# Attention and mixture of experts on one core: each head's k loaded on both halves of the rows, and q and k split in place

## The chip, the cores and the metric

The kernel runs on one core of a Trainium2 chip. The metric is the device time of one execution in microseconds; lower is better. Five engines work side by side, each through its own list of instructions in order: TensorE (PE, whose weight loads stand as PEld), VectorE (DVE), ScalarE (ACT), GpSimd (POOL), and SyncE (SP), which here issues nearly all DMAs. An instruction that waits for a semaphore holds up everything behind it on its engine.

## The reference

For 8 batches of 12 heads (448 positions, head size 64) a causal attention is computed in float32; its output, as 3584 rows of 768, goes to a mixture of 8 experts that picks one expert for each row and keeps the 80 rows with the largest gate for each.

```python
scores = scale * np.matmul(q, k.transpose(0, 1, 3, 2))
scores = np.where(mask, -1000000000.0, scores)
attn = np.exp(scores - np.max(scores, axis=-1, keepdims=True))
attn = attn / (np.sum(attn, axis=-1, keepdims=True) + 1e-09)
x = np.matmul(attn, v)            # then as (8 * 448, 768)
expert_idx = np.argmax(x @ w_gate, axis=1)
for e in range(8):
    tok_idx = the 80 rows of expert e with the largest gate_w
    out[tok_idx] = gate_w[tok_idx, None] * (np.maximum(x[tok_idx] @ w1[e], 0.0) @ w2[e])
```

## The kernel before

The heads are worked in **pairs**: 6 pairs in a batch, 48 in all, numbered 0 to 47 from here on. A pair has its even head's 64 components in SBUF rows 0 to 63 (`lo`) and its odd head's in rows 64 to 127 (`hi`). Loads and splits go by **thirds** of a batch, which are two pairs (`PH = 2`): 24 thirds. Third h is loaded two thirds ahead by `load_third` and split during third h-1 by the steps of `split_third`.

The splitting is there because a score is computed from float16 parts: q and k are each cut into a high part (the float16 rounding) and a low part (what is left). For the even head, `qa` holds q's high part in rows 0 to 63 and its low part in rows 64 to 127; `ka` holds k's high part in both halves, `la` k's low part in both halves. One matmul of `qa` with `ka` and one with `la` then give all four products. `qb`, `kb` and `lb` are the same for the odd head. These six tiles are double buffered.

In the kernel before, `by_dma` makes them so: ACT rounds q into `qh` (L331) and DVE rounds k into `kh` (L336), whole tiles of 128 rows by 896; DMAs inside SBUF copy the halves of `qh` to `qa` and `qb` (L332, L333) and those of `kh` twice each to `ka` and `kb` (L338, L339). POOL computes q's low parts from `qh` straight into `qa` and `qb` (L342, L343) and k's low part into `kl` (L347), and four more DMAs copy `kl` to `la` and `lb` (L351, L352). `qh`, `kh` and `kl` have one buffer each. The first pair of third 0 is split by `at_once` with compute instructions alone.

Each pair has 8 **slots**, and the order on every engine is written by hand. In slots 0 to 6 PE makes a block of scores (L375, L376; the last block L385 to L388), DVE masks it and takes the row minimum (L397), and ACT takes the exponential (L400); in slots 0, 2, 4 and 6 PE also transposes four blocks of the pair before (L417), which ACT or DVE copies out (L429). In slot 7 PE multiplies the transposed weights of two pairs before with v (L445). There are three score buffers and two transpose buffers in PSUM. A dictionary `plan` adds steps to the end of a slot: `THIRD` gives the slots of the split, counted from slot 1 of the first pair of a third, and `NORMS`, `ROWS0`, `ROWS1` and `STEPS` those of the gate and the choice of rows for the batch before, whose small operations run on POOL and DVE (for instance L625, which subtracts the largest logit, and L674, the one-hot rows that PE needs). `late_constants` puts a run of POOL instructions ahead of the split in pair 4.

After the last pair comes the choice for the last batch, then the two layers of the experts with weights streamed from HBM. SP issues in one list: the loads of q, k and v, the copies inside SBUF, the stores of attention rows (`xs`, L582), the weights that are loaded ahead (L189), and the zeroing of the output (`out<-zero`, L271).

Of the kernel before, what the change touches and what calls it, by code (L numbers as in the profile page):

```python
# [38 lines left out]
def attention_then_moe(  # L39
# [24 lines left out]
    assert NT == 4 and LAST == QB and D == NP * P  # L64
# [131 lines left out]
    wg_sb = const.tile([P, NP, E], F32, name="wg_sb")  # L196
    tiny = const.tile([P, 1], F32, name="tiny")
    nc.gpsimd.memset(tiny, 1e-9)
    lg = keep.tile([P, NT, H * E], F32, name="lg")
    if LAST < P:  # L200
        nc.vector.memset(lg[LAST:P, NT - 1, :], 0.0)

    def late_constants():
# [53 lines left out]
        zero = const.tile([P, D // 2], F32, name="zero")  # L257
        nc.gpsimd.memset(zero, 0.0)
# [41 lines left out]
    def split_third(h):  # L300
# [5 lines left out]
        one = lambda n: apool.tile([P, PH, S], F16, name=n, tag=n, bufs=1)  # L306
        for nm in ("qa", "qb", "ka", "kb", "la", "lb"):
            st[nm] = t16(nm)
        qa, qb, ka, kb, la, lb = (st[nm] for nm in ("qa", "qb", "ka", "kb", "la", "lb"))

        def at_once(x):

            nc.scalar.copy(ka[lo, x], kf[lo, x])
            nc.vector.tensor_copy(qa[lo, x], qf[lo, x])
            nc.scalar.copy(ka[hi, x], kf[lo, x])  # L315
            nc.vector.tensor_tensor(out=qa[hi, x], in0=qf[lo, x], in1=qa[lo, x], op=ALU.subtract)
            nc.scalar.copy(qb[hi, x], qf[hi, x])
# [2 lines left out]
            nc.scalar.copy(kb[hi, x], kf[hi, x])  # L320
            nc.scalar.copy(kb[lo, x], kf[hi, x])
            nc.vector.tensor_tensor(out=qb[lo, x], in0=qf[hi, x], in1=qb[hi, x], op=ALU.subtract)
            nc.vector.tensor_tensor(out=lb[lo, x], in0=kf[hi, x], in1=kb[hi, x], op=ALU.subtract)
            nc.vector.tensor_tensor(out=lb[hi, x], in0=kf[hi, x], in1=kb[hi, x], op=ALU.subtract)

        def by_dma(x):
            st["qh"], st["kh"] = qh, kh = one("qh"), one("kh")
            kl = one("kl")

            def q_hi():  # L330
                nc.scalar.copy(qh[:, x], qf[:, x])  # L331
                nc.sync.dma_start(qa[lo, x], qh[lo, x])  # L332
                nc.sync.dma_start(qb[hi, x], qh[hi, x])  # L333

            def k_hi():
                nc.vector.tensor_copy(kh[:, x], kf[:, x])  # L336
                for t, rows in ((ka, lo), (kb, hi)):
                    nc.sync.dma_start(t[lo, x], kh[rows, x])  # L338
                    nc.sync.dma_start(t[hi, x], kh[rows, x])  # L339

            def q_lo(i):
                nc.gpsimd.tensor_tensor(out=qa[hi, i], in0=qf[lo, i], in1=qh[lo, i], op=ALU.subtract)  # L342
                nc.gpsimd.tensor_tensor(out=qb[lo, i], in0=qf[hi, i], in1=qh[hi, i], op=ALU.subtract)  # L343

            def k_lo(i):
                eng = nc.gpsimd if h else nc.vector
                eng.tensor_tensor(out=kl[:, i], in0=kf[:, i], in1=kh[:, i], op=ALU.subtract)  # L347

            def spread():
                for t, rows in ((la, lo), (lb, hi)):  # L350
                    nc.sync.dma_start(t[lo, x], kl[rows, x])  # L351
                    nc.sync.dma_start(t[hi, x], kl[rows, x])  # L352
# [953 lines left out]
```

## Time and profile before

| what | us |
|---|---|
| median of 3 runs (lowest to highest) | 525.53 (523.63 to 528.52) |
| the profiled execution, its own time | 528.05 |
| its span, first to last instruction | 526.3 |
| PE busy in the span | 463.1 (88%) |
| DVE busy | 410.8 (78%) |
| ACT busy | 391.7 (74%) |
| POOL busy | 211.5 (40%) |

The shares are averages over stages that have different limits: the attention takes the first 365 us of the span, the choice for the last batch some 30, the experts the rest. TensorE's granted clock was 0.97 of full speed on average. The ends of matmuls are modelled, so a busy PE may still be waiting a little.

### The profile page before, as it was taken

The numbers are of one execution on the slowest core, as the hardware profiler recorded it, in microseconds if no ns is written. First come the engines' busy times: TensorE is split into PE (matmuls) and PEld (weight loads), VectorE is DVE, ScalarE is ACT, GpSimd is POOL, SyncE is SP. The second block draws the span as 40 slices with busy tenths as digits, with TensorE's granted clock in tenths as the row PEclk, the third lists the DMA queues.
The fourth block names the chain that finished last, engine by engine and source line by source line (L and its number), as shares of the span: only waits on it lengthen the run. The fifth ranks groups of instructions, "written<-read, shape, count | busy, mean of one in ns | idle before, by whom it ended". The sixth has DMA issues, their size and how long they took to land. (4 is left out here: it accounts for less than half of the span.)

```text
span 526.3 us, 14874 instructions
## 1 busy us (share of the span) xinstructions
PE 463.1 (88%) x5247; PEld 354.7 (67%) x5247; DVE 410.8 (78%) x1286; ACT 391.7 (74%) x1048; POOL 211.5 (40%) x294
## 2 busy tenths in 40 slices
PE   2687979979799999999999999999959898999985
PEld 1355736756576667667667667777547898999984
DVE  5566738866697798789889789889387999988771
ACT  4787748866687788788789778878164898978670
POOL 4477424544443654565445445460005155300010
PEclk9999879998899999999999999999978999999998
DMA  6775898788888888989988988983297999999920
GB/s 198 191 192 168 233 273 246 206 239 247 259 251 230 265 249 266 282 259 267 292 251 254 272 260 264 277 249 133 84 381 242 370 392 390 398 423 421 420 84 22
DMA packets 63947, 136.85 MB, mean 260 GB/s; under 512 B 8786, under 2 KB 50770, under 8 KB 60416
## 3 DMA queue, kind: packets, MB, share of 16 engines
q1 hardware_dynamic: 62816, 132.39, 78.1%
q0 software_dynamic: 1056, 3.51, 2.0%
q8 instruction: 41, 0.67, 0.5%
q14 instruction: 34, 0.28, 0.2%
HBM read 85.35 MB, written 23.99 MB: 208 GB/s over the span
## 5 line engine op out<-in xcount | busy, mean ns | idle before, releaser
L400 ACT ACTIVATE prob<-ns,nb 128x128 f32<-128x128 f32 (+3 forms) x336 | 176.9, 529 | 33.4 <-DVE nb L397 32.0
L397 DVE CUSTOM_DVE_ANT_0 ns<-sp,mask 128x384 f32<-128x384 f32 (+2 forms) x288 | 117.1, 416 | 57.9 <-PE sp L376 46.1
L417 PE MATMUL tp<-ident,prob 128*128 128x128 f32 x768 | 120.7, 281 | 0.8 <-ACT PT L429 0.7
L429 ACT COPY PT<-tp 128x512 f32<-128x512 f32 x144 | 82.9, 576 | 43.7 <-PE tp L417 29.3
L1083 DVE SCALAR_TENSOR_TENSOR wl<-wraw,wh 128x768 f16<-128x768 f32 (+1 forms) x94 | 93.8, 1062 | 11.4 <-ACT wh L1098 8.1
L417 PEld LDWEIGHTS tp<-ident,prob 128*128 128x128 f32 x768 | 91.0, 144 | 15.5 <-ACT PT L429 6.8
L342 POOL TENSOR_TENSOR qa<-qf,qh 64x448 f16<-64x448 f32 x47 | 49.1, 1045 | 123.4 <-ACT qh L331 115.1
L445 PE MATMUL xp<-PT,vt 128*64 128x448 f32 (+3 forms) x768 | 92.1, 380 | 0.0
L1098 ACT ACTIVATE wh<-wraw 128x768 f16<-128x768 f32 (+1 forms) x94 | 80.9, 923 | 5.5 <-DMA wraw<-w 1.8
L445 PEld LDWEIGHTS xp<-PT,vt 128*64 128x64 f32 x768 | 54.3, 137 | 43.6 <-issue 23.2
L1158 PEld LDWEIGHTS <-wl 128*128 128x128 f16 x640 | 64.4, 101 | 5.0 <-issue 3.1
L1155 PEld LDWEIGHTS <-wh 128*128 128x128 f16 x640 | 65.0, 102 | 3.5 <-issue 3.1
L1157 PEld LDWEIGHTS <-wh 128*128 128x128 f16 x640 | 64.5, 101 | 1.7 <-issue 1.6
L400 ACT ACTIVATION_READ_ACCUMULATOR prob<-ns,nb 128x1 f32 x336 | 63.9, 190 | 0.0
L376 PE MATMUL sp<-la,qa 128*128 128x128 f16 x144 | 40.7, 283 | 18.4 <-DMA la<-kl 18.0
L343 POOL TENSOR_TENSOR qb<-qf,qh 64x448 f16<-64x448 f32 x47 | 48.9, 1041 | 3.4
L1211 POOL DMA_INDIRECT out<-yo,idx x8 | 19.0, 2374 | 77.3 <-ACT yo L1208 67.4
L347 POOL TENSOR_TENSOR kl<-kf,kh 128x448 f16<-128x448 f32 x46 | 46.9, 1040 | 1.8
L375 PE MATMUL sp<-kb,qb 128*128 128x128 f16 x144 | 40.4, 280 | 7.2 <-DVE nb L397 6.4
L375 PE MATMUL sp<-ka,qa 128*128 128x128 f16 x144 | 40.8, 283 | 6.7 <-ACT ka L315 5.2
L376 PE MATMUL sp<-lb,qb 128*128 128x128 f16 x144 | 40.4, 281 | 5.5 <-DMA lb<-kl 4.5
L1158 PE MATMUL op<-hh,wl 128*128 128x80 f16 x336 | 39.4, 204 | 3.0 <-DVE wl L1083 1.5
(187 smaller groups left out, 952.2 us busy)
## 6 DMA issues: line engine op xcount, KB each, us to landing
wraw<-w SPq DMA_DIRECT2D x27, 1536.0 KB, 20.3
out<-zero SPq DMA_DIRECT2D x56, 192.0 KB, 2.4
qf<-q_t SPq DMA_DIRECT2D x23, 448.0 KB, 4.7
kf<-k_t SPq DMA_DIRECT2D x23, 448.0 KB, 6.1
vt<-v_t SPq DMA_DIRECT2D x24, 384.0 KB, 6.6
xs<-xr SPq DMA_DIRECT2D x48, 192.0 KB, 2.3
wraw<-w SPq DMA_DIRECT2D x24, 256.0 KB, 3.2
ka<-kh SPq DMA_DIRECT2D x46, 112.0 KB, 4.8
```

The costliest lines, as they stand in the source:

```text
L375: nc.tensor.matmul(sp[:, 0:w], qx[:, p, t * P:w], kx[:, p, 0:w], start=True, stop=False)
L376: nc.tensor.matmul(sp[:, 0:w], qx[:, p, t * P:w], lx[:, p, 0:w], start=False, stop=True)
L397: pr.masked = nc.vector.tensor_tensor_reduce(out=ns[:, 0:w], in0=sp[:, 0:w], in1=m, scale=-1.0 / 8.0, scalar=HUGE, op0=ALU.add, op1=ALU.mi ...
L400: nc.scalar.activation(pr.P[:, off:off + w], ns[:, 0:w], AF.Exp, bias=nb, scale=-1.0, accum_out=total)
L417: nc.tensor.transpose(pr.tp[:, i], pr.P[:, off:off + P], ident)
L429: copy(dst, src)
L445: state["pe"] = nc.tensor.matmul(xp[rows, 0:w], st["vt"][:, c, p * P + j * DH:p * P + (j + 1) * DH], pr.PT[:, j, n0:n0 + w], start=(c == 0 ...
L1083: return nc.vector.scalar_tensor_tensor(out=l, in0=src, scalar=SW, in1=h, op0=ALU.mult, op1=ALU.subtract)
L1098: nc.scalar.activation(h, src, AF.Copy, scale=SW)
L1155: nc.tensor.matmul(o, wh[:, ws], ah[:, c, :], start=(x == 0 and i % per == 0), stop=False, skip_group_check=True)
L1157: nc.tensor.matmul(o, wh[:, ws], al[:, c, :], start=False, stop=False, skip_group_check=True)
L1158: nc.tensor.matmul(o, wl[:, ws], ah[:, c, :], start=False, stop=(x == n - 1), skip_group_check=True)
```

## The change

k is loaded twice: `kfa` holds the even head's k in both halves of the rows and `kfb` the odd head's, by four loads of 64 rows where there was one of 128. q's high part is rounded by ACT straight into its place in `qa` and `qb` (two instructions of 64 rows by 896 instead of one of 128 rows). DVE rounds `kfa` into `ka` and `kfb` into `kb` (two instructions of 128 by 896 instead of one). POOL subtracts `la` and `lb` in full (two instructions of 128 by 448 for each pair instead of one). The ten copies by DMA inside SBUF and the tiles `qh`, `kh` and `kl` are gone. The order of the steps is now q's low part, then k's low part, for the first pair of the third, and then the same for its second pair. The numbers in `THIRD` move with it; two transposes of rows (`ROWS1`), the first step of `NORMS` and one of `STEPS` move by a few slots. `wg_sb` becomes a view of `lg`, `zero` a view of `mask_l`.

```diff
-NORMS = [1, 2, 2]
+NORMS = [0, 2, 2]
...
-ROWS1 = [59, 62, 64, 67]
+ROWS1 = [59, 65, 65, 67]
...
-THIRD = [0, 0, 2, 3, 4, 6, 8]
+THIRD = [1, 1, 2, 2, 4, 5, 8]
...
-        zero = const.tile([P, D // 2], F32, name="zero")
-        nc.gpsimd.memset(zero, 0.0)
+        zero = mask_l[:, 0:D // 2]
...
-        st["qf"], st["kf"] = qf, kf = t32("qf"), t32("kf")
+        st["qf"], st["kf"] = qf, kf = t32("qf"), [t32("kfa"), t32("kfb")]
...
             nc.sync.dma_start(qf[:, x], qT[b, :, ps, :])
-            nc.sync.dma_start(kf[:, x], kT[b, :, ps, :])
+            for j, rows in enumerate((lo, hi)):
+                nc.sync.dma_start(kf[j][lo, x], kT[b, rows, ps, :])
+                nc.sync.dma_start(kf[j][hi, x], kT[b, rows, ps, :])
...
-        def by_dma(x):
-            st["qh"], st["kh"] = qh, kh = one("qh"), one("kh")
-            kl = one("kl")
...
+        def by_turns(x):
+            def q_high():
+                nc.scalar.copy(qa[lo, x], qf[lo, x])
+                nc.scalar.copy(qb[hi, x], qf[hi, x])
+
+            def k_high(j):
+                nc.vector.tensor_copy(k_hi[j][:, x], kf[j][:, x])
+
+            def q_low(i):
+                nc.gpsimd.tensor_tensor(out=qa[hi, i], in0=qf[lo, i], in1=qa[lo, i], op=ALU.subtract)
+                nc.gpsimd.tensor_tensor(out=qb[lo, i], in0=qf[hi, i], in1=qb[hi, i], op=ALU.subtract)
+
+            def k_low(i):
+                for j in range(2):
+                    nc.gpsimd.tensor_tensor(out=k_lo[j][:, i], in0=kf[j][:, i], in1=k_hi[j][:, i], op=ALU.subtract)
             each = range(x.start, x.stop)
-            return [q_hi, k_hi] + [lambda i=i: q_lo(i) for i in each] + [lambda i=i: k_lo(i) for i in each] + [spread]
+            return [q_high, lambda: k_high(0), lambda: k_high(1)] + [f for i in each
+                                                                    for f in (lambda i=i: q_low(i), lambda i=i: k_low(i))]
```

`at_once` changes in the same way: three casts on ACT instead of five, and one cast and four subtractions on DVE instead of one and six.

How the order of the instructions moves is shown at three places. The first is SP's list from the load of one third to the copies of `kl`, in the second batch (before: 12 rows, the last being the first of the four copies of `kl`):

```order
L288 DMA qf<-q_t 128x896
L289 DMA kf<-k_t 128x896
L296 DMA vt_107<-v_t 128x3x256
L298 DMA vt_107<-v_t 64x256
L332 DMA qa<-qh 64x896
L333 DMA qb<-qh 64x896
L338 DMA ka<-kh 64x896
L339 DMA ka<-kh 64x896
L338 DMA kb<-kh 64x896
L339 DMA kb<-kh 64x896
L189 DMA wraw<-w 128x512 x2
L351 DMA la<-kl 64x896
```

The same place after:

```order
L287 DMA qf<-q_t 128x896
L289 DMA kfa<-k_t 64x896
L290 DMA kfa<-k_t 64x896
L289 DMA kfb<-k_t 64x896
L290 DMA kfb<-k_t 64x896
L297 DMA vt_107<-v_t 128x3x256
L299 DMA vt_107<-v_t 64x256
L189 DMA wraw<-w 128x512 x4
```

Of a third's SP instructions ten copies have gone and three loads have come; no part of the split is left in this list.

The second place is ACT in pair 4, where third 3 is split: `prob` is the exponential, `PT` the copy of transposes, `qh` or `qa` and `qb` q's high part. Before:

```order
L400 ACTIVATE prob_101,sums<-ns,nb 128x128 x2
L331 CAST qh<-qf 128x896
L429 COPY PT<-tp 128x2x2x128
L400 ACTIVATE prob_101,sums<-ns,nb 128x256 x2
L429 COPY PT<-tp 128x2x256
```

After:

```order
L386 ACTIVATE prob_101,sums<-ns,nb 128x128 x2
L415 COPY PT<-tp 128x2x2x128
L386 ACTIVATE prob_101,sums<-ns,nb 128x256
L325 CAST qa<-qf 64x896
L326 CAST qb<-qf 64x896
L386 ACTIVATE prob_101,sums<-ns,nb 128x256
L415 COPY PT<-tp 128x2x256
```

The rounding of q moves one slot later and is two instructions. DVE's casts of k move likewise: the first to slot 2, the second to slot 3, each behind that slot's masking.

The third place is POOL in the second batch, where a third's split meets the first steps of the gate (`gsh` from the logits, `ggw` the weights), from q's low part of the third's second pair on. Before:

```order
L342 TENSOR_TENSOR qa<-qf,qh 64x448
L343 TENSOR_TENSOR qb<-qf,qh 64x448
L347 TENSOR_TENSOR kl<-kf,kh 128x448 x2
L625 TENSOR_TENSOR gsh<-logit,gmx 128x32
L645 TENSOR_SCALAR ggw<-ggw 128x4
```

After:

```order
L332 TENSOR_TENSOR qa<-qf,qa 64x448
L333 TENSOR_TENSOR qb<-qf,qb 64x448
L611 TENSOR_TENSOR gsh<-logit,gmx 128x32
L337 TENSOR_TENSOR la<-kfa,ka 128x448
L337 TENSOR_TENSOR lb<-kfb,kb 128x448
L631 TENSOR_SCALAR ggw<-ggw 128x4
```

The gate's first step now stands ahead of k's low part for the second pair, and six subtractions stand ahead of it, as before (two of them, k's low part of the first pair, are not among the rows shown). PE's first matmul of a third waits for the subtractions of its own pair alone, no longer for the whole third.

## Rows read from the trace of the kernel before

**Rows 1.** Windows by batch: length, PE PEld DVE ACT POOL, clock, DMA, GB/s

```profile
5.19:49.85 44.66, 32.80 (x241) 21.09 (x240) 30.14 (x102) 34.11 (x105) 30.26 (x49) 1.00 0.69 197
49.85:100.97 51.12, 42.86 (x343) 29.66 (x339) 32.93 (x124) 35.70 (x112) 21.20 (x30) 0.90 0.82 231
100.97:152.16 51.19, 43.75 (x370) 31.55 (x366) 36.76 (x143) 35.82 (x110) 21.40 (x31) 0.93 0.83 245
...
195.85:239.26 43.41, 41.18 (x377) 29.26 (x374) 36.86 (x144) 35.71 (x110) 21.44 (x31) 1.00 0.88 263
239.26:281.82 42.56, 40.77 (x377) 29.09 (x374) 36.68 (x144) 35.54 (x110) 21.36 (x31) 1.00 0.89 267
```

**Rows 2.** Waits of PE, whole span: for whom, us in total, times, longest

```profile
PE sp L376 <- DMA la<-kl: 18.0, 11, 3.8
```

**Rows 3.** Waits of PE, the first 46 us

```profile
PE sp L376 <- DMA la<-kl: 1.2, 2, 0.8
PE sp L375 <- DMA ka<-kh: 1.1, 1, 1.1
...
PE sp L376 <- DMA lb<-kl: 0.9, 2, 0.5
```

**Rows 4.** Waits of PE from 152 to 365 us (the last five batches)

```profile
PE sp L376 <- DMA la<-kl: 3.5, 5, 0.9
PE sp L376 <- DMA lb<-kl: 2.7, 8, 0.7
```

**Rows 5.** PE's timeline, pair 14: start, duration, what, [idle before <-releaser]

```profile
118.76 0.29 PE L376 MATMUL sp<-la,qa 128*128 128x128 f16 x1 [3.44 <-DMA la<-kl]
...
121.02 1.06 PE L417 MATMUL tp<-ident,prob 128*128 128x128 f32 x4
...
124.61 0.60 PE L417 MATMUL tp<-ident,prob 128*128 128x128 f32 x4
```

**Rows 6.** Timelines of POOL and SP, ahead of pair 14

```profile
109.19 2.04 POOL L347 TENSOR_TENSOR kl<-kf,kh 128x448 f16<-128x448 f32 x2
...
114.17 0.45 SPq L582 DMA_DIRECT2D xs<-xr  x1
114.71 0.47 SPq L351 DMA_DIRECT2D la<-kl  x1
```

**Rows 7.** Groups by line and form: count, busy us, mean ns of one, idle before

```profile
L342 POOL TENSOR_TENSOR qa<-qf,qh 64x448 f16<-64x448 f32 x47 | 49.1, 1045 | 123.4 <-ACT qh L331 115.1 <-issue 6.6
...
L347 POOL TENSOR_TENSOR kl<-kf,kh 128x448 f16<-128x448 f32 x46 | 46.9, 1040 | 1.8
...
L331 ACT CAST qh<-qf 128x896 f16<-128x896 f32 x23 | 21.3, 924 | 1.6 <-DMA qb<-qh 1.6
...
L336 DVE CAST kh<-kf 128x896 f16<-128x896 f32 x23 | 15.3, 666 | 3.6 <-DMA kb<-kh 3.5
...
L331 ACT CAST qh<-qf 128x448 f16<-128x448 f32 x1 | 0.6, 564 | 0.0
...
L317 ACT CAST qb<-qf 64x448 f16<-64x448 f32 x1 | 0.6, 561 | 0.0
```

**Rows 8.** Timeline of all engines, pair 0

```profile
13.94 1.02 POOL L342 TENSOR_TENSOR qa<-qf,qh 64x448 f16<-64x448 f32 x1 [2.69 <-ACT qh L331]
14.09 1.35 DVE L336 CAST kh<-kf 128x896 f16<-128x896 f32 x1 [3.51 <-DMA kb<-kh]
...
15.04 1.30 POOL L343 TENSOR_TENSOR qb<-qf,qh 64x448 f16<-64x448 f32 x1
...
15.84 0.48 PE L375 MATMUL sp<-kb,qb 128*128 128x384 f16 x1 [4.19 <-DVE nb L397]
```

**Rows 9.** Timeline of POOL, pairs 4 and 5

```profile
43.63 1.04 POOL L342 TENSOR_TENSOR qa<-qf,qh 64x448 f16<-64x448 f32 x1
...
48.07 2.04 POOL L347 TENSOR_TENSOR kl<-kf,kh 128x448 f16<-128x448 f32 x2
```

**Rows 10.** Busy time in the first 10 us

```profile
0.00:10.00 10.00, 1.49 (x6) 0.78 (x7) 6.62 (x12) 4.57 (x7) 4.95 (x18) 1.00 0.75 238
```

More of the change, by code (lines that the diff above doesn't have):

```diff
@@ L27 @@
 TSLOT = [0, 2, 4, 6]
-NORMS = [1, 2, 2]
+NORMS = [0, 2, 2]
 ROWGAP = 1
 ROWS0 = [2, 3, 7, 13]
-ROWS1 = [59, 62, 64, 67]
-STEPS = {'gp': 18, 'gs': 19, 'lp': 21, 'lg': 22, 'logit': 22, 'shifted': 25, 'chosen': 26, 'sums': 27, 'one_hot': 28, 'weight': 28, 'weighted': 31, 'columns': 30, 'parts': 33, 'r0t': 32, 'r0c': 33, 'r1t': 34, 'r1c': 35, 'rl': 36, 'lt': 36, 'c3w': 37, 'c3l': 38, 'cp': 40, 'ro': 41, 'c2w': 41, 'c2l': 43, 'c1w': 43, 'c1l': 44, 'c0w': 45, 'c0l': 46, 'places': 47, 'gt': 47, 'earlier': 51, 'own': 47, 'rank': 51, 'rr': 51, 'tn': 54, 'tab': 54, 'rp': 56, 'row': 58}
+ROWS1 = [59, 65, 65, 67]
+STEPS = {'gp': 18, 'gs': 19, 'lp': 21, 'lg': 22, 'logit': 22, 'shifted': 25, 'chosen': 26, 'sums': 27, 'one_hot': 28, 'weight': 28, 'weighted': 31, 'columns': 30, 'parts': 33, 'r0t': 32, 'r0c': 33, 'r1t': 34, 'r1c': 35, 'rl': 36, 'lt': 36, 'c3w': 37, 'c3l': 38, 'cp': 40, 'ro': 41, 'c2w': 41, 'c2l': 43, 'c1w': 43, 'c1l': 44, 'c0w': 45, 'c0l': 46, 'places': 47, 'gt': 47, 'earlier': 51, 'own': 47, 'rank': 51, 'rr': 51, 'tn': 54, 'tab': 55, 'rp': 56, 'row': 58}
 EARLY = {'gp': 19, 'gs': 19, 'lp': 21, 'lg': 21, 'logit': 22, 'shifted': 24, 'chosen': 25, 'sums': 26, 'one_hot': 27, 'weight': 28, 'weighted': 29, 'columns': 28, 'parts': 30, 'r0t': 30, 'r0c': 31, 'r1t': 32, 'r1c': 33, 'rl': 34, 'lt': 35, 'c3w': 35, 'c3l': 36, 'cp': 38, 'ro': 39, 'c2w': 39, 'c2l': 39, 'c1w': 40, 'c1l': 40, 'c0w': 40, 'c0l': 41, 'places': 42, 'gt': 42, 'earlier': 43, 'own': 42, 'rank': 45, 'rr': 46, 'tn': 48, 'tab': 50, 'rp': 51, 'row': 52}
 ROWS_EARLY = [22, 25, 27, 44]
-THIRD = [0, 0, 2, 3, 4, 6, 8]
+THIRD = [1, 1, 2, 2, 4, 5, 8]
 @with_exitstack
@@ L63, in attention_then_moe @@
     CAP = max(0, min(int(capacity), N))
-    assert NT == 4 and LAST == QB and D == NP * P
+    assert NT == 4 and LAST == QB and D == NP * P and D // 2 <= S - LAST
     const = ctx.enter_context(tc.tile_pool(name="const", bufs=1))
@@ L194, in attention_then_moe @@
     identb = before = dec = number = number_after = pnum = tbase = wgd = slots_e = slots_t = zero = zdone = xg_bufs = None
-    wg_sb = const.tile([P, NP, E], F32, name="wg_sb")
     tiny = const.tile([P, 1], F32, name="tiny")
@@ L199, in attention_then_moe @@
     lg = keep.tile([P, NT, H * E], F32, name="lg")
+    wg_sb = lg[:, 0, 0:NP * E].rearrange("k (p e) -> k p e", e=E)
     if LAST < P:
@@ L305, in split_third @@
         t16 = lambda n: apool.tile([P, PH, S], F16, name=n, tag=n)
-        one = lambda n: apool.tile([P, PH, S], F16, name=n, tag=n, bufs=1)
         for nm in ("qa", "qb", "ka", "kb", "la", "lb"):
             st[nm] = t16(nm)
-        qa, qb, ka, kb, la, lb = (st[nm] for nm in ("qa", "qb", "ka", "kb", "la", "lb"))
+        qa, qb, k_hi, k_lo = st["qa"], st["qb"], (st["ka"], st["kb"]), (st["la"], st["lb"])
         def at_once(x):
-            nc.scalar.copy(ka[lo, x], kf[lo, x])
+            sub = lambda o, a, b: nc.vector.tensor_tensor(out=o, in0=a, in1=b, op=ALU.subtract)
+            nc.scalar.copy(k_hi[0][:, x], kf[0][:, x])
@@ L314, in at_once @@
             nc.vector.tensor_copy(qa[lo, x], qf[lo, x])
-            nc.scalar.copy(ka[hi, x], kf[lo, x])
-            nc.vector.tensor_tensor(out=qa[hi, x], in0=qf[lo, x], in1=qa[lo, x], op=ALU.subtract)
+            sub(qa[hi, x], qf[lo, x], qa[lo, x])
             nc.scalar.copy(qb[hi, x], qf[hi, x])
-            nc.vector.tensor_tensor(out=la[lo, x], in0=kf[lo, x], in1=ka[lo, x], op=ALU.subtract)
-            nc.vector.tensor_tensor(out=la[hi, x], in0=kf[lo, x], in1=ka[lo, x], op=ALU.subtract)
@@ L320, in at_once @@
[L320 to L324, printed above, removed]
-        def by_dma(x):
-            st["qh"], st["kh"] = qh, kh = one("qh"), one("kh")
-            kl = one("kl")
[L330 to L352, printed above, removed]
@@ new lines, in at_once @@
+            sub(k_lo[0][:, x], kf[0][:, x], k_hi[0][:, x])
+            nc.scalar.copy(k_hi[1][:, x], kf[1][:, x])
+            sub(qb[lo, x], qf[hi, x], qb[hi, x])
+            sub(k_lo[1][:, x], kf[1][:, x], k_hi[1][:, x])
+        def by_turns(x):
[10 more added lines that the diff above has]
+                    nc.gpsimd.tensor_tensor(out=k_lo[j][:, i], in0=kf[j][:, i], in1=k_hi[j][:, i], op=ALU.subtract)
@@ L360, in attention_then_moe @@
+        return by_turns(slice(0, PH))
     class Pair:
```

4 lines of the change are left out of this document (1 added, 3 removed).

## The prediction

> **What bounds the kernel now.** I read the busy time by batch first. In batches 4 and 5 (the two beside them are alike) PE is busy 41.2 of 43.4 us and 40.8 of 42.6 us at the full clock, DVE 36.9 and 36.7, ACT 35.7 and 35.5, POOL 21.4 [rows 1]. So PE paces the settled attention, with some 2 us to be had in a batch. Batches 1 and 2 do the same work but take 51.1 and 51.2 us, at a granted clock of 0.90 and 0.93 [rows 1]; batch 0, which has no gate of a batch before to work on, takes 44.7 us with PE busy for only 32.8 of them [rows 1].
>
> PE's waits say why. The largest is for `la`, which a DMA copies from `kl`: 18.0 us in 11 waits [rows 2]. Pair 14 shows a long one: PE stands 3.44 us until `la` has landed, and afterwards four transposes take 1.06 us where 3.6 us later they take 0.60 [rows 5]: after the standstill TensorE runs at the lower of its two levels (1.2 against 2.4 GHz) before it is back. That copy is not late because POOL is late: POOL ended `kl` at 111.2 us (109.19 + 2.04), but SP issued the copy at 114.71, behind the stores of `xs` [rows 6], and PE stood from 118.76 - 3.44 = 115.32 on [rows 5]. PE thus waits for SP's list and a transfer, not for arithmetic. This wait ends last at the first pair of a third, so a change to it reaches the end of the attention. The experts after it, and the choice before them, keep their instructions, so I carry the gain through to the end unchanged.
>
> **The copies go: gain.** Three terms, by stretches that don't overlap.
>
> Batches 1 and 2 against the mean of batches 4 and 5 (43.0 us): 51.1 + 51.2 - 86.0 = 16.3 us [rows 1]. I take all of it: it is the four long waits, of which rows 5 show one, plus the slow clock behind each.
>
> Short waits for `la` and `lb` remain in the settled batches too: 3.5 + 2.7 = 6.2 us over the last five batches [rows 4], 1.24 in a batch. They go from all seven batches behind batch 0 (batches 1 and 2 were brought down only to a batch that still has them): 8.7 us.
>
> Batch 0: PE's waits for copies are 1.2 + 1.1 + 0.9 = 3.2 us [rows 3]. Besides, PE stands for 4.19 us because DVE stands for 3.51: `kh` has one buffer, and its copies to `kb` must land before third 1 may be rounded [rows 8]. Without `kh` there is nothing of that kind, so 4.2 us more. Against it stands k's second load: two thirds of 0.46 MB more in the first stretch, where the core moves 238 GB/s at a DMA share of 0.75 [rows 10]. At that rate, in full on the path, 0.92 MB would be 3.9 us; hidden it is 0. The queue is not full and the copies it competed with are gone, so I take 1.0. Batch 0 gains 3.2 + 4.2 - 1.0 = 6.4 us.
>
> Sum of gains: 16.3 + 8.7 + 6.4 = 31.4 us.
>
> **The added work: cost.** In each third but the first ACT has one more cast. One of 128 by 448 takes 564 ns and one of 64 by 448 takes 561, so half the rows save nothing, and each of the two costs 924 ns: +0.92 us [rows 7]. DVE has one more cast of 128 by 896: +0.67 us [rows 7]. POOL has two more subtractions, of 1.04 us each [rows 7]: +2.08. On 23 thirds. A batch of three thirds would then have DVE at 36.9 + 2.0 = 38.9 us and ACT at 35.7 + 2.8 = 38.5, both still under PE's 41.2 [rows 1]. The work that hides them is PE's own. It doesn't hide them fully, since they come in a lump in slots 2 and 3 of the first pair, and what is queued behind them is the masking on DVE, and the exponentials and copies of transposes on ACT, for which PE waits when its three score buffers or two transpose buffers are used up. From below the cost is 0 (the engine sums); I see no reason for less, as nothing of this work gets shorter. From above it is DVE's cast plus one POOL instruction that it stands behind, 0.67 + 1.04 = 1.71 us a third [rows 7]. I take 0.25, near the lower end because of the 2.3 us that each batch leaves between DVE or ACT and PE: 23 x 0.25 = 5.8 us.
>
> POOL: eight subtractions a third at the spacing of (48.07 - 43.63) / 4 = 1.11 us [rows 9] are 8.9 us, of the some 14 us that two pairs take. That is covered in the settled batches, the more so as PE's first matmul waits for the first four alone. The gate's steps wait behind six subtractions, as before. In batch 0 it is not covered: POOL was busy 30.3 of 44.7 us [rows 1]; eight more subtractions (one of them formerly DVE's) make 38.6, and the batch is to take 38.3. The run of constants puts POOL at third 3 only at 43.63 [rows 9], and pair 6 would now be there at about that time. Between 0 and the four subtractions of its own pair (4.4 us) I take 1.5, nearer to 0 since each earlier third also comes to POOL sooner.
>
> SP loses ten issues of about half a microsecond a third and gains three; it gives PE nothing to wait for, so 0. The moved transposes (`ROWS1`), `NORMS` and `STEPS` shift the same work between neighbouring pairs: 0.
>
> **Sum.** -31.4 + 5.8 + 1.5 = -24.1 us. The profiled execution took 528.05, which gives 503.9; it stood 2.5 us above the median of the runs shown (525.53), so I forecast 501.4, say **501 us**.
>
> **The rivals.**
>
> *ACT sets the pace of a third's first pair.* Then ACT's second cast is paid in full: 23 x 0.92 = 21.2 us in place of 5.8, a gain of 8.7 and a time of 517. For it: ACT works in order and the casts are one block of 1.85 us. Against it: by batch it is busy 5.5 us less than PE [rows 1]. Chance 0.13.
>
> *POOL comes late.* The stall changes its name from the copy to POOL's subtraction, and half of the 16.3 us in batches 1 and 2 stays: 8.2 us, time 509.5. For it: the full POOL of batch 0. Against it: `kl` was ready 3.5 us before its copy was issued [rows 6]. Chance 0.12.
>
> *Slower: DVE stands behind POOL.* In pair 0 a cast of k that began 0.15 us after a POOL subtraction took 1.35 us, twice the mean of 0.67, and the next POOL subtraction, begun while that cast still ran, took 1.30 instead of 1.04 [rows 7, 8]: one of them waits for the other. Now two casts, one of them a slot later, stand against eight POOL instructions. If in every third one cast stands behind a POOL instruction, and DVE's 1.71 us land on the path, 23 of them cost 39.3 us against 31.4 - 1.5 of gain: +9.4, a time of 535. It turns into a loss from 29.9 / 23 = 1.3 us a third. Against it: the mean over all 23 casts is 0.67 [rows 7], so most stood behind nothing, and POOL starts only behind ACT's first cast, when DVE's first has usually ended. Chance 0.06. The Trainium skill, in SBUF — State Buffer, section "SBUF: two separate sides", speaks for this rival: it calls the port pair that VectorE and GpSimd share "an exclusive lock, not a bandwidth split", held for a whole instruction. The two rows of pair 0 agree; by that rule the cost would be at the upper end wherever the casts meet POOL.
>
> *The copies' waits are hidden anyway.* PE would find the next thing late at once, and the time stays within 1% (524). Against it: behind the waits of PE for `la` there is a clock loss that nothing else makes, and DVE and ACT idle in just these batches. Chance 0.07.
>
> *More than forecast.* All lumps are hidden: 528.05 - 31.4 - 2.5, or 494 and less. Chance 0.05.
>
> **How the numbers follow.** The forecast has the remaining 0.57, with 494 to 508 as its own range. A measurement of this kernel tells about 1% from no change. Faster by more: forecast, ACT, POOL and more-than-forecast, 0.87; within 1%: 0.07; slower: 0.06. For 8 in 10 the range takes in the forecast, POOL's case, and about half each of ACT's and of the better one: 492 to 516.
>
> **What would show it.** Right: no wait of PE for a DMA into `la` or `lb`; batches 1 and 2 at 41 to 44 us and at the full clock; no wait of 4 us in pair 0; ACT some 21 us and DVE some 15 us busier, POOL some 48. Wrong: waits of PE for POOL's `la` at the start of thirds (POOL's case); DVE's casts of k at 1.3 us or more (the lock); settled batches above 43 us with ACT near 40 (ACT's case). The forecast fails altogether if the experts' stage starts earlier but ends at the same time, because something there waits for a transfer that the earlier start doesn't bring forward.

## The result and the profile after

The changed kernel takes 508.75 us (median of 4 runs, lowest 507.67), the kernel before beside it 525.11 (523.63 to 528.52): ratio 0.967, 95% interval 0.961 to 0.974. The forecast was 501, its range 492 to 516. So the sign of the gain and its largest term came out as worked out, and 7.7 us of the gain are missing. The profiled run took 509.36 (span 507.7, before 526.3). One execution of after, at 516.22, ran at a lower granted clock and is left out of the ratio; so are such executions of the kernels below, where the lowest time stands beside the median if they differ much.

The windows by batch, as in [rows 1] (length, then PE, PEld, DVE, ACT, POOL busy, granted clock, DMA share, GB/s), here batches 0, 1, 2, 4, 5 and 7:

```profile
6.56:49.22 42.66, 33.77 (x241) 21.68 (x240) 30.19 (x103) 37.00 (x108) 33.92 (x52) 1.00 0.71 183
49.22:90.62 41.40, 38.80 (x342) 27.31 (x339) 35.69 (x127) 38.27 (x115) 32.96 (x40) 1.00 0.86 247
90.62:133.60 42.98, 40.96 (x370) 29.12 (x366) 39.35 (x146) 38.26 (x113) 27.78 (x37) 1.00 0.82 233
...
176.87:219.87 43.00, 41.07 (x378) 29.31 (x374) 39.61 (x147) 38.29 (x113) 28.23 (x38) 1.00 0.74 217
219.87:262.86 42.99, 41.06 (x378) 29.21 (x375) 39.61 (x147) 38.31 (x113) 28.22 (x38) 1.00 0.75 217
...
305.85:347.90 42.05, 39.78 (x373) 29.41 (x371) 38.65 (x148) 35.25 (x108) 20.74 (x31) 1.00 0.51 156
```

Batches 1 and 2 have come down from 51.1 and 51.2 us to 41.4 and 43.0, at the full clock. Batches 4 and 5 stay where they were (43.4 and 42.6 before), and batch 7 got longer (40.51 before). Batch 0 ends at 49.22 where it ended at 49.85. Profiled run against profiled run:

| stretch | forecast, us | measured, us |
|---|---|---|
| to the end of batch 0 | -6.4 + 1.5 + 3 x 0.25 = -4.2 | 49.22 - 49.85 = -0.6 |
| batches 1 and 2 | -16.3 - 2 x 1.24 + 6 x 0.25 = -17.3 | 84.4 - 102.3 = -17.9 |
| batches 3 to 7 | -5 x 1.24 + 14 x 0.25 = -2.7 | 214.3 - 213.0 = +1.3 |
| behind the attention | 0 | 159.8 - 161.1 = -1.3 |
| sum | -24.1 | -18.6 |

By medians it is 16.4, since the profiled run of before stood 2.9 us above its median and that of after 0.6.

The largest waits of PE, whole span (for whom, us in total, times, longest); [rows 2] is gone:

```profile
PE sp L361 <- ACT ka L314: 6.6, 1, 6.6
PE tp L403 <- ACT prob L386: 4.5, 16, 0.9
PE gp L481 <- DVE xr L564: 3.8, 5, 0.8
PE selt L682 <- DVE oh L660: 3.2, 1, 3.2
PE sp L361 <- DVE nb L383: 3.1, 2, 1.8
```

No DMA into `la` or `lb` is among them, nor POOL with a term worth naming. New is the wait of the gate's product `gp` for `xr`, 3.8 us in 5 waits, one in each of batches 2 to 6.

The forms that answer to [rows 7] (count, busy us, mean ns, idle before):

```profile
L325 ACT CAST qa<-qf 64x896 f16<-64x896 f32 x23 | 21.4, 931 | 0.2
L326 ACT CAST qb<-qf 64x896 f16<-64x896 f32 x23 | 21.5, 936 | 0.6
L329 DVE CAST kb<-kfb 128x896 f16<-128x896 f32 x23 | 18.7, 813 | 1.2 <-DMA kfb<-k_t 1.2
L329 DVE CAST ka<-kfa 128x896 f16<-128x896 f32 x23 | 14.8, 645 | 2.3 <-DMA kfa<-k_t 2.3
...
L618 DVE SCALAR_TENSOR_TENSOR goh<-gsh,dec 128x32 f32<-128x32 f32 x8 | 7.3, 919 | 0.3 <-POOL gsh L611 0.2
```

ACT's added cast costs what was worked out (0.93), DVE's second one 0.81 instead of 0.67. The last row is a small step of the gate that the forecast has no term for. Before, it took 186 ns:

```profile
L632 DVE SCALAR_TENSOR_TENSOR goh<-gsh,dec 128x32 f32<-128x32 f32 x8 | 1.5, 186 | 0.0
```

It follows POOL's `gsh`, behind which POOL now goes straight on to k's low part. In batch 4 it began at 202.93 us, just behind the start of such a subtraction (202.88 to 203.92), and took 1.03 us. None of PE's waits names it.

The start, from the timeline of all engines (start, duration, what, [idle before <- releaser]):

```profile
4.65 1.28 ACT L314 ACT_TABLE_LOAD   x1 [4.65 <-DMA kfa<-k_t]
5.95 0.56 ACT L314 CAST ka<-kfa 128x448 f16<-128x448 f32 x1
6.56 0.27 PE L361 MATMUL sp<-ka,qa 128*128 128x128 f16 x1 [6.56 <-ACT ka L314]
8.30 1.07 POOL L332 TENSOR_TENSOR qa<-qf,qa 64x448 f16<-64x448 f32 x1 [4.80 <-ACT qa L325]
8.39 1.23 DVE L329 CAST ka<-kfa 128x448 f16<-128x448 f32 x1
9.54 1.22 DVE L329 CAST kb<-kfb 128x448 f16<-128x448 f32 x1
...
11.02 0.37 PE L361 MATMUL sp<-kb,qb 128*128 128x256 f16 x1 [1.80 <-DVE nb L383]
...
13.78 0.63 DVE L329 CAST ka<-kfa 128x896 f16<-128x896 f32 x1 [2.26 <-DMA kfa<-k_t]
14.80 0.53 PE L371 MATMUL sp<-ka,qa 128*64 128x448 f16 x1 [1.92 <-DVE nb L383]
```

DVE's long stand of [rows 8] for `kh` is gone, but others stand here. ACT's table load, which began at 0.79 us before, now stands behind the load of `kfa`. DVE waits for third 1's loads while its masking is queued behind that cast. SP issued third 1's `kfa` at 7.43 and 7.94 us, where it issued third 1's `kf` at 3.12 before: seven more issues, of some 0.6 us each, stand ahead of it in the list. And two casts of 128 by 448 take 1.23 and 1.22 us beside POOL, where one of double the size takes 0.63 (13.78 us); that is not new in kind, since the one such cast before took 1.11 us there.

### The profile page after: what moved, and what is told of

It is laid out like the page before. It is cut to its first block, busy times and chain, and to the rows that moved or that the text cites. A ratio compares the mean times of both kernels' runs of the same rounds, so it can differ in the third digit from the quotient of the medians.

```text
span 507.7 us, 14728 instructions
## 1 busy us (share of the span) xinstructions
PE 457.5 (90%) x5247; PEld 351.2 (69%) x5247; DVE 428.8 (84%) x1307; ACT 410.7 (81%) x1070; POOL 269.7 (53%) x341
## 5 line engine op out<-in xcount | busy, mean ns | idle before, releaser
L403 PEld LDWEIGHTS tp<-ident,prob 128*128 128x128 f32 x768 | 89.0, 142 | 24.2 <-ACT prob L386 11.9
L1069 DVE SCALAR_TENSOR_TENSOR wl<-wraw,wh 128x768 f16<-128x768 f32 (+1 forms) x94 | 93.7, 1060 | 10.3 <-ACT wh L1084 7.9
L332 POOL TENSOR_TENSOR qa<-qf,qa 64x448 f16<-64x448 f32 x47 | 49.2, 1046 | 80.9 <-ACT qa L325 48.0
L1197 POOL DMA_INDIRECT out<-yo,idx x8 | 22.2, 2781 | 72.9 <-ACT yo L1194 63.0
L333 POOL TENSOR_TENSOR qb<-qf,qb 64x448 f16<-64x448 f32 x47 | 48.6, 1035 | 8.4 <-DMA nowhere<-w,none 5.1
L337 POOL TENSOR_TENSOR la<-kfa,ka 128x448 f16<-128x448 f32 x47 | 50.7, 1079 | 3.1
L337 POOL TENSOR_TENSOR lb<-kfb,kb 128x448 f16<-128x448 f32 x47 | 49.6, 1056 | 0.0
L1141 PE MATMUL op<-hh,wh 128*128 128x80 f16 x336 | 39.5, 205 | 1.4 <-issue 1.1
L1144 PE MATMUL op<-hh,wl 128*128 128x80 f16 x336 | 39.4, 205 | 1.5 <-DVE wl L1069 1.5
```

What stands on the lines that cost most here:

```text
L337: nc.gpsimd.tensor_tensor(out=k_lo[j][:, i], in0=kf[j][:, i], in1=k_hi[j][:, i], op=ALU.subtract)
L403: nc.tensor.transpose(pr.tp[:, i], pr.P[:, off:off + P], ident)
L1069: return nc.vector.scalar_tensor_tensor(out=l, in0=src, scalar=SW, in1=h, op0=ALU.mult, op1=ALU.subtract)
L1141: nc.tensor.matmul(o, wh[:, ws], ah[:, c, :], start=(x == 0 and i % per == 0), stop=False, skip_group_check=True)
L1144: nc.tensor.matmul(o, wl[:, ws], ah[:, c, :], start=False, stop=(x == n - 1), skip_group_check=True)
```

## The experiments

My theory after the result: the long waits went as forecast; in the settled batches the collision of two transposes of rows in one slot took the gain back; in batch 0 new waits at the start did. The rivals: the casts added on ACT or on DVE pace the thirds now; DVE stands behind POOL.

**Rows in four slots again** (on the changed kernel):

```diff
-ROWS1 = [59, 65, 65, 67]
+ROWS1 = [59, 62, 64, 67]
```

> The changed kernel with one table put back as it was before the change: the transposes of the attention's rows stand in four different slots again, where the change put two of them into one slot, so that the two buffers of PSUM that they share with the gate's product fill up at once. In the settled batches of the changed kernel PE waits 0.76 us a batch for such a buffer, the longest wait that is left there. If that collision stands on the path, the time falls by 7 x 0.76 = 5 us, to about 503.5, and the settled batches from 43.0 to 42.3. If DVE (or ACT) paces these batches, the wait only changes its name: 507.5 to 510, no wait of PE for xr, and batches still at 43.0. If the move was needed for something that I have not seen, it gets slower.

Measured 503.68 (503.40 to 504.96); ratio to before 0.960 (0.952 to 0.968). First what happened in the changed kernel, PE and DVE in pair 14:

```profile
105.04 0.82 PE L558 MATMUL rt<-ident,xu 128*128 128x128 f32 x6
...
107.28 1.70 PE L481 MATMUL gp<-xu,wgd 128*32 128x448 f32 x12 [0.76 <-DVE xr L564]
...
106.58 1.01 DVE L564 TENSOR_TENSOR xr<-rt,sums 128x384 f32<-128x384 f32 x2
```

Both groups of rows are transposed in one go, fill the two buffers that `gp` needs as well, and DVE empties them only behind its masking. With the table put back, the windows of batches 4 and 5 are

```profile
175.57:217.79 42.22, 40.72 (x377) 29.35 (x374) 39.60 (x147) 38.13 (x113) 28.22 (x38) 1.00 0.77 221
217.79:259.98 42.19, 40.70 (x377) 29.34 (x374) 39.60 (x147) 38.13 (x113) 28.20 (x38) 1.00 0.77 221
```

0.8 us less a batch, as expected, in batches 2 to 6; batch 1 became 0.5 us longer. The attention's last pair begins 3.7 us earlier (342.7 to 339.0). The rest of the 5.1 us lies behind the attention, where this edit moves nothing: the experts took 116.6 us in this run and 118.5 in that of after, at clocks of 1.00 and 0.99 (rows further down). That the total met the expected 503.5 is thus in part luck. PE's longest wait in batches 4 to 6 is now that of `lp`, a later product of the gate, for ACT's `gs`: 2.5 us in 3 waits, where after had 0.8.

**k's casts one slot earlier**:

```diff
-THIRD = [1, 1, 2, 2, 4, 5, 8]
+THIRD = [1, 0, 1, 2, 4, 5, 8]
```

> The changed kernel with the two roundings of k on DVE one slot earlier, so that they mostly end before POOL begins its run of subtractions. In the changed kernel the rounding into ka takes 645 ns on average and that into kb 813, up to 1.43 us when a subtraction of POOL runs beside it. If standing behind POOL is what costs the settled batches their gain, kb comes down to about 650 ns and the time by up to 23 x 0.17 = 4 us, and by more if POOL's subtractions also begin earlier: 503 to 507. If PE or ACT paces these batches, kb gets shorter but the time stays at 507.5 to 510. If the roundings stand in the way of the masking instead, later work is late: 510 or more.

Measured 511.18 (lowest 509.75). k's second cast, the window of batch 4, and DVE in pair 1:

```profile
L329 DVE CAST kb<-kfb 128x896 f16<-128x896 f32 x23 | 14.0, 608 | 0.5 <-DMA kfb<-k_t 0.5
...
178.72:221.74 43.02, 40.47 (x378) 29.13 (x375) 38.48 (x147) 38.39 (x113) 27.93 (x38) 1.00 0.75 217
...
14.47 0.63 DVE L329 CAST ka<-kfa 128x896 f16<-128x896 f32 x1 [3.20 <-DMA kfa<-k_t]
```

The cast into `kb` came down from 813 to 608 ns, so it had stood behind POOL, and the settled batches stayed at 43.0: in this kernel, which still has the collision, that stand is not on their path. What got longer is batch 0, 44.93 us for 42.66; there the cast now waits 3.20 us for third 1's load, 0.9 more, with all masking behind it.

**A dose on ACT** (q's second cast twice in every third but the first) and **a dose on DVE** (k's second cast twice), each alone:

```diff
-                nc.scalar.copy(qb[hi, x], qf[hi, x])
+                for _ in range(2 if h else 1):
+                    nc.scalar.copy(qb[hi, x], qf[hi, x])
```

```diff
-                nc.vector.tensor_copy(k_hi[j][:, x], kf[j][:, x])
+                for _ in range(2 if h and j else 1):
+                    nc.vector.tensor_copy(k_hi[j][:, x], kf[j][:, x])
```

> The changed kernel with q's second rounding on ACT done twice in every third but the first: a dose of 0.92 us for ACT in 23 thirds, 21.2 us in all, with nothing else moved. If ACT paces a third's first pair, most of it comes out in the time: 15 to 21 us more, 524 to 530. If PE or DVE paces there, 0 to 6 us more, 509 to 515. It measures the price of the very instruction that the change added on ACT, for which my forecast took part of 0.25 us a third (6 us in all).

> The changed kernel with k's second rounding on DVE done twice in every third but the first: a dose of 0.65 to 0.81 us for DVE in 23 thirds, 15 to 19 us in all. If DVE paces the settled batches now (its busy time in the three pairs that are laden with the gate's steps equals their length), it comes out nearly in full: 12 to 19 us more, 521 to 528. If PE paces them, 0 to 4 us more, 509 to 513. The two doses together say which engine the added work of the change is paid on.

Measured 524.16 (+15.4) and 520.69 (+11.9). A settled batch of the dose on ACT, then one of the dose on DVE with its casts:

```profile
185.21:229.91 44.70, 40.85 (x378) 29.24 (x375) 39.02 (x147) 40.84 (x116) 27.36 (x37) 1.00 0.73 209
```

```profile
183.07:227.94 44.87, 41.67 (x377) 29.08 (x374) 41.23 (x150) 38.30 (x113) 29.11 (x38) 1.00 0.73 208
...
L330 DVE CAST kb<-kfb 128x896 f16<-128x896 f32 x46 | 39.4, 857 | 1.8 <-DMA kfb<-k_t 1.0
```

A batch grew by 1.7 us for 3 x 0.92 = 2.8 on ACT, and by 1.9 for 2.7 on DVE (39.4 less 18.7 us of casts, on 23 thirds: 0.90 each). Both engines pay more than 60% of what is added. Read alone, each dose would say that its engine paces; the removals below measure the other direction.

**ACT's table at once**: a copy of one column of `prob` onto itself, ahead of the first loads.

```diff
+        x = prob[0][:, OFF_L + S:OFF_L + S + 1]
+        nc.scalar.copy(x, x)
         for h in range(2):
             load_third(h)
```

> The changed kernel with one tiny copy on ACT (one column of prob onto itself) ahead of the loads. In the changed kernel the load of ACT's table begins at 4.65 us, where before it began at 0.79, and the first matmul at 6.56 in place of 5.19: the load stands behind the wait for the first tile of k. If the table then loads while k is on its way, the first matmul comes at 5.2 to 5.4 us and the time falls by 1.2 to 1.4 us, to about 507.4. If the loads of k end last anyway, first matmul at 6.2 or later and the time within 0.4 us of 508.75.

```profile
0.79 1.28 ACT L916 ACT_TABLE_LOAD   x1 [0.79 <-PEq L1286]
2.08 0.19 ACT L916 COPY prob<-prob 128x1 f32<-128x1 f32 x1
...
5.30 0.27 PE L361 MATMUL sp<-ka,qa 128*128 128x128 f16 x1 [5.30 <-ACT ka L314]
```

The first matmul comes at 5.30 us for 6.56, and the last pair of the attention begins 1.3 us earlier (341.4). The time is 508.07 (lowest 507.21); the difference of 0.7 by itself is within the measurement, the shift of the trace is not.

**Third 1 split three slots later**:

```diff
-        third_plan(1, 1)
+        third_plan(1, 4)
```

> The changed kernel with the split of third 1 put three slots later within the first pairs. In the changed kernel DVE there stands 2.3 and 1.2 us for the loads of kfa and kfb (k is loaded twice now, and they land at about 13.7 and 15.9 us), and PE stands 1.9 and 1.3 us behind DVE's masking. If the wait for the second load is what took back the gain that I forecast for batch 0, its end moves from 49.2 to 46 or 47 us and the time falls by 2 to 3 us, to about 506. If ACT's or POOL's work paces batch 0 (ACT busy for all of pairs 3 and 5), the waits vanish from pair 0 and come back later: batch 0 ends at 48.5 to 50, time 508 to 509.5. If POOL then comes too late for pair 2, slower: 510 or more.

Measured 508.18 (lowest 505.21). Batches 0 and 1:

```profile
6.43:47.31 40.88, 34.22 (x241) 22.31 (x240) 30.45 (x103) 36.96 (x108) 32.56 (x50) 1.00 0.73 192
47.31:90.07 42.76, 39.03 (x342) 27.36 (x339) 35.73 (x127) 38.28 (x115) 34.27 (x42) 1.00 0.83 239
```

Batch 0 gains 1.8 us, batch 1 gives 1.4 back. New waits of PE for POOL's `la` (0.9 and 1.1 us) stand at the start of thirds 1 and 3, so POOL is the next late thing there.

**The kernel before, with the copies of `kl` issued by POOL** instead of SP, all four in a third:

```diff
-                    nc.sync.dma_start(t[lo, x], kl[rows, x])
-                    nc.sync.dma_start(t[hi, x], kl[rows, x])
+                    nc.gpsimd.dma_start(t[lo, x], kl[rows, x])
+                    nc.gpsimd.dma_start(t[hi, x], kl[rows, x])
```

> The kernel before, with nothing changed but the queue that issues the four copies of kl to la and lb in a third: POOL issues them, right behind the subtractions that make kl, in place of SP, where they stand behind stores and loads of weights. All copies remain. If SP's list made them late, as I argued for pair 14, the long waits of PE for la go, batches 1 and 2 fall from 51.1 and 51.2 us to 43 to 45 at the full clock, and the time to 509 to 514. If the transfers themselves are slow because the queues of data are full, or if POOL is late, the batches stay at 48 or more and the time at 519 to 527.

Measured 579.9 (lowest 567.27): the expected gain did not come, and the time lies far outside the rival's range as well. PE's waits, and one of them in the timelines of POOL and PE:

```profile
PE sp L376 <- DMA la<-kl: 51.3, 15, 10.0
...
60.10 0.56 POOL L351 DMA_DIRECT2D la<-kl  x1 [0.30 <-POOL kl L347]
...
67.99 0.29 PE L376 MATMUL sp<-la,qa 128*128 128x128 f16 x1 [7.87 <-DMA la<-kl]
```

Issued 0.30 us behind `kl`, the copy reached PE 7.9 us later. The DMA views of this kernel and of before (KB each, median us from issue to landing):

```profile
la<-kl POOLq DMA_DIRECT2D x46, 112.0 KB, 4.1
```

```profile
la<-kl SPq DMA_DIRECT2D x46, 112.0 KB, 2.3
```

Past SP's list the copies start earlier, but then run beside the loads of q, k and v that SP issued from 58.48 to 60.73 us. The DMA share was 1.00, 0.91 and 1.08 in the three stretches of 2 us from 60 us on, and this third's copies took 6.6 us to `la` and 7.2 to `lb` (medians). In the kernel before, the copies that SP issues right behind those loads are slow as well: a median of 4.8 us for `ka` and 5.6 for `qa`, of the same size. The run changes both the moment and the queue and doesn't separate them. Nor does it show when pair 14's copy would have landed had SP issued it at once. The Trainium skill, in DMA: Bandwidth & Descriptors, section "Issuing engines are not separate DMA queues", says that transfers of all issuing engines end on the same 16 DMA engines and interleave. The run agrees in that the other queue gave nothing (579.9 us for 525.4). Of the 54.7 us between the two profiled runs (spans of 581.0 and 526.3), PE's longer waits for `la` make 33.3 (51.3 for 18.0), and the granted clock had fallen to 0.50 by the end of the wait shown; the rest stays open. What removed the wait, in the changed kernel, was having no copy.

**The kernel before with two buffers for `kh`**; room comes from making `wg_sb` and `zero` views, as in the change.

```diff
-            st["qh"], st["kh"] = qh, kh = one("qh"), one("kh")
+            st["qh"], st["kh"] = qh, kh = one("qh"), t16("kh")
```

> The kernel before, with two buffers for kh in place of one (the room comes from the two views that the change introduces as well). It tests one term of my sum by itself: that DVE's wait of 3.51 us for the copies out of kh, and PE's of 4.19 us behind it in pair 0, is worth 4.2 us. If so, batch 0 ends at about 45.6 us in place of 49.85 and the time falls by some 4 us, to 522. If PE then stands for the next late thing (the copies, the table of constants, ACT or POOL), batch 0 ends at 48.5 or later and the time falls by 0 to 1.3 us: 525 to 526.5.

Batches 0 and 1 and the experts, and the experts in before, after and with the rows back, in this order:

```profile
5.16:46.68 41.52, 33.45 (x240) 21.42 (x240) 29.56 (x102) 34.11 (x105) 29.89 (x48) 1.00 0.73 211
46.68:96.40 49.72, 40.64 (x342) 28.18 (x339) 32.68 (x124) 35.62 (x112) 20.91 (x29) 0.93 0.81 237
...
395.48:518.04 122.56, 115.28 (x2262) 113.09 (x2263) 102.60 (x117) 93.76 (x147) 27.23 (x13) 0.94 0.84 334
```

```profile
400.04:519.93 119.89, 110.76 (x2262) 108.33 (x2263) 102.76 (x117) 93.49 (x147) 29.34 (x13) 0.99 0.87 342
```

```profile
382.76:501.23 118.47, 110.49 (x2262) 108.31 (x2263) 102.11 (x117) 92.69 (x147) 33.50 (x13) 0.99 0.87 345
```

```profile
378.96:495.54 116.58, 109.38 (x2262) 106.77 (x2263) 102.41 (x117) 92.85 (x147) 33.95 (x13) 1.00 0.89 351
```

Batch 0 ends 3.2 us earlier, where I had put 4.2. PE's waits for DVE's masking there fell by 4.0 us (6.4 to 2.4), and 0.5 came back as waits for copies (3.2 to 3.7). Yet the time is 529.44 (10 runs, 525.58 to 531.97), ratio 1.009 (1.005 to 1.013). In the profiled run (526.19) the last pair begins 5.2 us earlier than before (360.0 to 354.8), and the experts, untouched, took 122.6 us at a clock of 0.94; the longer runs have no trace, so what they lost is not shown. Four kernels with the same experts spend 116.6 to 122.6 us on them, the longest at the lowest granted clock and the shortest at the highest. A gain of some microseconds in the attention can be lost or doubled there, and is read from the trace, not from the total.

**Three edits together** (rows in four slots, the table at once, third 1 later, by their diffs above):

> Three of the edits together on the changed kernel: the transposes of rows back in four slots, the tiny copy that lets ACT's table load at once, and the split of third 1 three slots later. Alone they took 3.7, 1.3 and 0.5 us off the attention. If they are independent (the first acts in every batch, the second at the very start, the third in batches 0 and 1), the attention is 5.5 us shorter and the time 502 or a little less. If the table's gain is eaten by the wait for third 1's loads, which land when they land, 503 to 504, no better than the first edit alone (503.68).

Measured 503.98 (503.25 to 505.33). Batch 0:

```profile
5.30:47.47 42.17, 33.31 (x240) 21.69 (x240) 30.27 (x103) 36.95 (x108) 32.41 (x50) 1.00 0.74 193
```

The last pair begins at 338.1, 0.9 us before that with the rows alone (339.0), not 1.8: with the earlier start, the later split gains nothing. At the end of batch 0 the table alone gave 1.5 us (49.22 to 47.73) and the split alone 1.9 (49.22 to 47.31); the two together give 1.6 (49.05 with the rows alone, to 47.47). So they do not add.

**A cast taken away from ACT, or from DVE, and given to POOL**, each on the changed kernel with the rows in four slots:

```diff
-                nc.scalar.copy(qb[hi, x], qf[hi, x])
+                cast = nc.gpsimd.tensor_copy if h else nc.scalar.copy
+                cast(qb[hi, x], qf[hi, x])
```

```diff
-                nc.vector.tensor_copy(k_hi[j][:, x], kf[j][:, x])
+                eng = nc.gpsimd if h and j else nc.vector
+                eng.tensor_copy(k_hi[j][:, x], kf[j][:, x])
```

> The changed kernel with the transposes of rows back in four slots, and besides q's second rounding (into qb) done by POOL in place of ACT in every third but the first. It takes away from ACT just the cast that the change added, 0.92 us in 23 thirds; POOL pays for it, at an estimate two of its subtractions of 64 by 448, 2.1 us. The dose of one more such cast cost 15.4 us. If ACT's load is paid in the same measure downward, the time falls by up to 15 us; PE is busy 40.7 of 42.2 us in the settled batches, so no more than 1.5 us a batch can go there: 494 to 500. If ACT's cast is hidden now and only more of it shows, 502 to 505. If POOL comes late with q's low parts for its longer list, PE waits for qa, la or lb: 506 or more.

> The changed kernel with the transposes of rows back in four slots, and besides k's second rounding (into kb) done by POOL in place of DVE in every third but the first. It takes away from DVE the cast that the change added, 0.67 to 0.81 us in 23 thirds, and its meeting with POOL's subtractions; POOL pays at an estimate two of its subtractions, 2.1 us. The dose of one more such cast cost 12 us. If DVE's load is paid in the same measure downward, 495 to 500, with settled batches near 41. If it is hidden now, 502 to 505. If POOL comes late, 506 or more. Of this run and the one with q's rounding on POOL, the one that gains names the engine on which the change's added work is still paid.

With q's cast on POOL: 514.25, lowest 507.35, both above the 503.68 of the rows alone. Batch 1, a settled batch, POOL's cast, PE's waits:

```profile
50.93:96.01 45.08, 40.67 (x339) 29.32 (x340) 35.92 (x127) 35.49 (x110) 37.58 (x44) 0.92 0.78 223
...
179.52:221.42 41.90, 40.61 (x377) 29.27 (x374) 39.38 (x147) 35.51 (x110) 31.01 (x41) 1.00 0.77 223
...
L327 POOL CAST qb<-qf 64x896 f16<-64x896 f32 x23 | 24.4, 1060 | 7.7 <-DMA nowhere<-w,none 6.2
...
PE sp L363 <- POOL la L338: 3.9, 2, 2.0
PE sp L362 <- POOL qa L333: 3.2, 1, 3.2
```

With k's cast on POOL: 507.10 (505.62 to 512.49), a settled batch:

```profile
176.28:218.36 42.08, 40.64 (x377) 29.04 (x374) 37.64 (x144) 38.01 (x113) 30.59 (x41) 1.00 0.77 222
```

Of the 42.2 us of a settled batch, 0.3 go with ACT's 2.8 us of cast, and 0.1 with DVE's 2.4, each net of what the same cast costs on POOL. So each cast is nearly hidden while the other stands. PE's waits fit that: without ACT's cast, PE's wait of `lp` for `gs` in batches 4 to 6 falls from 2.5 us to 0.8, and two new ones for DVE come up (0.6 us each); without DVE's, the 2.5 stay. What both together would give was not run. In batches 0 and 1 POOL has no room: PE waits 7.1 us for it in the first of the two kernels and 2.7 in the second.

**Put together**: rows in four slots, the table at once, and q's second cast on POOL from third 8 on.

```diff
-ROWS1 = [59, 65, 65, 67]
+ROWS1 = [59, 62, 64, 67]
...
-                nc.scalar.copy(qb[hi, x], qf[hi, x])
+                cast = nc.gpsimd.tensor_copy if h > 7 else nc.scalar.copy
+                cast(qb[hi, x], qf[hi, x])
...
+        x = prob[0][:, OFF_L + S:OFF_L + S + 1]
+        nc.scalar.copy(x, x)
```

> A version put together from what the runs before it showed, on the changed kernel: the transposes of rows back in four slots, the tiny copy that lets ACT's table load at once, and q's second rounding on POOL from third 8 on, where POOL has room (in batches 0 and 1 that cast made PE wait for POOL's qa and la, in batches 2 to 6 it took 0.3 us off each). The split of third 1 stays where the change put it. If the three are independent: 503.7 - 1.3 - 5 x 0.3 = 500.9 us, the first matmul at 5.3, settled batches at 41.9. If the earlier start is given back because third 1's loads land no earlier, 502 to 502.5. If POOL falls behind anywhere, 504 or more, and PE's waits name POOL.

Measured 502.79 (6 runs, 501.27 to 505.81), ratio to before 0.955 (0.950 to 0.960): faster than the kernel before, and 1.2% under the changed one (its longest run, 505.81, lies below the shortest of that, 507.67). The expected 500.9 was not reached. The settled batches are at 41.9 us and the last pair begins at 336.4, 2.6 us before that with the rows alone; of the 1.3 us at the start only 0.4 are left at the end of batch 0 (49.05 to 48.66). That the total fell by 0.9 only lies behind the attention: from the start of the last pair to the end it took 164.3 us, with the rows alone 163.0. PE waits for none of POOL's casts or subtractions of the split.

## Why the prediction came out as it did

**Batches 1 and 2: right in place and mechanism, and in size with some luck.** 17.9 us against 17.3. The waits for copies and the low clock behind them went together. By the sum each batch would come to 43.0 - 1.24 + 0.75 = 42.5 us. Batch 1 came to 41.4, because it doesn't do quite the same work as a settled one (PE busy 38.8 us for 41.1; [rows 1] has 343 instructions of PE for 377); batch 2 came to 43.0, since it pays the collision below.

**My reason for the copy's lateness: not borne out.** I wrote that PE waits for "SP's list and a transfer". With POOL's queue in place of SP's list the copies got slower, so the transfer is the larger part at least there; how much of pair 14's wait was the list stays open. The forecast did not hang on this, since the change removes the copies altogether; a forecast for another queue would have been far off.

**Batches 3 to 7: the step that failed** is "The moved transposes (`ROWS1`), `NORMS` and `STEPS` shift the same work between neighbouring pairs: 0". Put back, `ROWS1` gives 0.8 us in a batch. The mean of batches 3 to 6 is 43.1 before, 43.1 after and 42.3 with the rows back: a gain of 0.9 where I had 1.24 - 0.75 = 0.5 net. So the short waits did pay, and the collision took it. Batch 7 is 1.5 us longer after, and only 0.1 of it goes with the rows; it stands in its third and fourth pairs (8.45 to 9.63 us and 6.46 to 7.20), and what makes it stays open.

**The added casts: somewhat less than forecast, as far as shown.** If the two removals add up, they give 0.3 + 0.1 = 0.4 us a batch, about 0.14 a third against my 0.25. It fits that 43.1 - 1.24 + 0.4 gives the 42.3 measured; but one engine may hide the other's cost, and removing both was not run. The rival "ACT sets the pace" falls: its 0.92 us a third would be 2.8 a batch, and the settled batches with the rows back are shorter than before. The dose shows how near it was. "POOL comes late" falls too: PE's waits for POOL's `lb` are 0.2 us in the whole span of after. "DVE stands behind POOL" is right as a mechanism (813 ns for 608, and the gate's step at 919 for 186), and for the casts not on the path of the settled batches.

**Batch 0: mis-sized, 0.6 for 4.2.** Of the 3.5 us that are missing, the table load behind the wait for k and the split of third 1 took 1.5 and 1.9 one by one, and 1.6 together (with the rows back); most of the split's part was paid back in batch 1 (1.4). My 1.0 for the extra load was a share of a transfer. It left out that the extra loads keep third 1's back in SP's list (I had put SP at 0), and that DVE's masking is queued behind a cast that waits for them. `kh`'s buffer was worth 3.2 for 4.2, in a kernel where the copies were still there to wait for; without them the 4.2 may hold. So some 2 us stay open. POOL, for which PE waits as soon as the split moves, and the casts beside it are candidates that no run separates.

**Busy time.** ACT rose by 19.0 us, DVE by 18.0 and POOL by 58.2, where I had put 21, 15 and 48; of POOL's, 53.4 are the subtractions of k.

**Behind the attention**: carried through "unchanged" in the forecast; the 1.3 us of gain there in the profiled runs lie in the experts (119.9 to 118.5 us), which the change doesn't touch; the granted clock reads 0.99 in both, so what made it is not shown.

## What to carry to other kernels

Removing a stall that also drops the clock was worth the whole excess of its batches here (17.9 us, forecast 17.3); take that from the windows by stage. But cost every moved line of a slot table by the buffers it shares: two users of two PSUM buffers in one slot took back 0.8 us in a batch. And a dose is no price: adding a cast cost 60 to 70% of its length, taking one away on one engine gave about 10% or less, so measure in the direction in which you mean to go, and remember that with two engines near the path taking from one does not say what taking from both would give.

## What the runs showed of the hardware

- The load of ACT's table can stand behind what its first instruction waits for. After, where that waits for two loads of `kfa`, it began at 4.65 us; before, where that waits for one load, at 0.79. Whether the number of loads decides was not tested. A tiny copy ahead brought it back to 0.79 and the first matmul 1.3 us forward. The Trainium skill, in ScalarE: Activation LUTs, section "What ACT_TABLE_LOAD costs", gives about 1283 ns for the load and about 1380 for a drain behind it. The load agrees (1.28); at this first load no drain is seen, the copy behind it began at 2.08, just when the load ended.
- DVE's cast of 128 by 448 took 1.23 and 1.22 us beside POOL's subtractions, while one of twice the size took 0.63 alone. A DVE step of 128 by 32 with two inputs took 919 ns on average where a subtraction of POOL ran beside it, and 186 before.
- POOL rounds 64 by 896 in 1060 ns, and 128 by 896 in 930 (k's cast, mean of 23): no more than one of its subtractions of half that length (1046), and half of what I had estimated.
